# Columns 32 to 39 of the chunk rows: a second fetch from DRAM against a copy by ScalarE

## The chip, the cores and the metric

The kernel runs on one core of one Trainium2 chip. The metric is the device time of one execution in microseconds (us), the median of the runs that were timed. The core has five engines with an instruction stream each: TensorE (PE, with its weight loads as PEld), VectorE (DVE), ScalarE (ACT), GpSimd (POOL) and SyncE (SP). Each works through its own stream in order; an instruction that waits for another engine, or for a DMA, holds up all that stands behind it in its stream. SP computes nothing here: it issues nearly all of the DMAs.

## The reference

Two parts follow each other: a linear-attention recurrence over 768 steps with a 40 by 40 state for each of 4 x 8 heads, and a two-layer block on its output.

```python
for t in range(S):                       # S = 768, for every batch b and head h
    y[:, :, t] = np.einsum('bhd,bhde->bhe', rt, state)
    Sa = np.einsum('bhde,bhe->bhd', state, at)
    state_decay = state * wt[:, :, None, :] - np.einsum('bhd,bhe->bhde', Sa, bt)
    state = state_decay + np.einsum('bhd,bhe->bhde', vt, kt)
x = y.transpose(0, 2, 1, 3).reshape(B * S, H * D)      # 3072 x 320
h = x @ w_in                                            # 320 x 2048
g = np.where(h >= 1, h, np.where(h <= -1, 0.0, (h + 1) ** 2 / 4))
out = g @ w_out                                         # 2048 x 320
```

## The kernel before

**Recurrence in chunks.** The 768 steps are cut into 24 chunks of 32 (`L = 32`, `D = 40`, 32 heads). Everything that a chunk needs stands in one row of 240 numbers for each head and step in a DRAM scratch, `scr`: r, v, k, the running decay P, a and b, 40 columns each (`O_R`, `O_V`, `O_K`, `O_P`, `O_A`, `O_B`). There are six scratch tensors, for 128 steps (a set of four chunks) each. For the first two sets the rows are made at the start (`early_rows`, `early_store`), for the others by `prelude` in the background, in four parts a set: ScalarE copies (`wz`, `arena`), VectorE scans, GpSimd products, and a DMA of 640 KB from `arena` to `scr`, after which the next part may write `arena` again.

**From rows to columns.** The products want the 40 numbers of a row on 40 partitions. VectorE transposes blocks of 32 by 32, so 40 numbers take two blocks: columns 0 to 31 of a block of 40 go to partitions 0 to 31, and columns 32 to 39 to partitions 32 to 39. For that, `load_rows` puts each row into SBUF twice. The 32 steps of the heads with f = 0 lie on partitions 0 to 31, and once more on partitions 32 to 63, there from column 32 on, so that the same 32-column window of the tile that shows columns 0 to 31 on the first 32 partitions shows columns 32 to 63 on the next. The heads with f = 1 lie likewise on partitions 64 to 95 and 96 to 127. That makes four DMAs a call: for each f one of n columns (q = 0), and one of n - 32 columns (q = 1). `load_ti` calls it for the tile `ti` (columns 0 to 199 of 16 heads, so a half chunk, `hb` 0 or 1; two tiles, one for each `hb`) and `ab_set` for columns a and b of all 32 heads, from set 2 on (tile `tiab`, and for set 2 `lw` as a second buffer).

**The consumers.** `turn(c, hb, part)` transposes `ti` into `cg` (L464), `ev` (L467) and `pr` (L469). `ab_set` transposes into `ea` (L328), whose products (L337) ScalarE copies to `pairs` (L343); `invert(s)` makes of them the inverses that set s needs.

**The order.** The main loop runs over the chunks. A pass has four parts; each begins with `stage` calls (one step of the chain of a half chunk: L519, L523; L529, L536, L540; L545 to L569; L585, L587, L575) and ends with `fill()`. `fill` hands out, by fixed rates written at the top, MoE matmuls (`feed`: first layer L631, gate L639 to L642, split L648 and L649, second layer L661), the conversion of the weights (`wgen`) and the background (`rows`, `ab`, `inv`, by the table WINDOWS). So each engine's stream is fixed when the program is built. `load_ti(c + 2, 0)` stands in the last part of pass c, and `turn(c + 2, 0, 0)` in the second part of pass c + 1; for hb = 1 load and turn are half a pass apart as well.

```python
    def load_ti(c, hb):
        drain("rows", c // 4)
        tis[c, hb] = tih[hb]
        load_rows(tih[hb], c, 0, 200, 16 * hb, 16)
```

`pad_rows` zeroes, on ScalarE, the 32 columns at the end of the second copies, which no DMA writes: of both `ti` tiles at the start, and of `tiab` before set 2.

Of the kernel before, what the change touches and what calls it, by code (L numbers as in the profile page):

```python
# [22 lines left out]
RW = 240  # L23
# [31 lines left out]
def rwkv_moe_kernel(ctx: ExitStack, tc: tile.TileContext, r, k, v, w, a, b, w_in, w_out, ident_d, mask_d, out):  # L55
    nc = tc.nc
# [29 lines left out]
    tiab = const.tile([128, 16, 80], F32, name="tiab")  # L86
# [31 lines left out]
    def zero(x, row=0):  # L118
        z = zero_c[row : row + x.shape[0]]
        nc.scalar.copy(x, (z if len(x.shape) == 2 else z.unsqueeze(1)).broadcast_to(list(x.shape)))  # L120

    def pad_rows(x, n):
        for q in (1, 3):
            zero(x[32 * q : 32 * q + 32, :, n : n + 32], 32 * q)

    def init_cg(i, part):
        cg, pr = cgs[i], prs[i]
# [175 lines left out]
    def load_rows(dst, c, off, n, h0=0, nh=NH):  # L303

        sc = scr[c // 4]
        for f in range(2):
            for q in range(2):
                row = (h0 + f) * 128 + 32 * (c % 4)
                m = n - 32 * q
                src = bass.AP(  # L310
                    sc.tensor, sc.offset + row * RW + off + 32 * q, [[RW, 32], [256 * RW, nh // 2], [1, m]]
                )
                nc.sync.dma_start(dst[64 * f + 32 * q : 64 * f + 32 * q + 32, :, 0:m], src)  # L313

    def ab_set(s):

        if s == 2:
            pad_rows(tiab, 48)
        bufs = [tiab, lw[:, 0:1280].rearrange("p (h x) -> p h x", x=80)] if s == 2 else [tiab]
        for c in range(4 * s, 4 * s + len(bufs)):  # L320
            load_rows(bufs[c % len(bufs)], c, O_A, 80)
        yield AB_W[5]
        for c in range(4 * s, 4 * s + 4):
            tv = bufs[c % len(bufs)].rearrange("p h (j x) -> p h j x", x=40)[:, :, :, 0:32]
            for half in range(2):
                ea = work.tile([128, 8, 2, 32], F32, tag="ea", name="ea")
                for i in range(2):
                    nc.vector.transpose(ea[:, 4 * i : 4 * i + 4], tv[:, 8 * half + 4 * i : 8 * half + 4 * i + 4])  # L328
                    yield AB_W[0]
                yield AB_W[1]  # L330
                ps = psum()[:, 0:128]
                for p in range(8):
                    for f in range(2):
                        rows = slice(64 * f, 64 * f + D)
                        q = 2 * f + p % 2
                        sl = p // 2
                        nc.tensor.matmul(  # L337
                            ps[32 * q : 32 * q + 32, 32 * sl : 32 * sl + 32],
                            lhsT=ea[rows, p, 0, :], rhs=ea[rows, p, 1, :], start=True, stop=True,
                        )  # L340
                assert s - 1 in turned_in
                at = 256 * (c % 4) + 128 * half
                nc.scalar.copy(pairs_f[:, at : at + 128], ps)  # L343
                yield AB_W[2] + AB_W[3]
            if c + len(bufs) < 4 * s + 4:
                load_rows(bufs[c % len(bufs)], c + len(bufs), O_A, 80)
            if c < 4 * s + 3:
                yield AB_W[4] // len(bufs)
# [26 lines left out]
    def adopt(s):  # L375

        drain("inv", s)
        W = lw[:, 1024:2048]
        nc.vector.transpose(tinv.rearrange("p c h i -> p i (c h)"), W.rearrange("p (a i) -> p i a", i=32))
        turned_out.add(s)  # L380
# [50 lines left out]
    tis = {}  # L431
# [5 lines that stand above are left out]
# [16 lines left out]

    quarter = lambda f, i: slice(64 * (1 - f) + 32 * i, 64 * (1 - f) + 32 * i + 32)
    order = [4 * (n % 2) + n // 2 for n in range(8)]

    def turn(c, hb, part):
        u = 2 * c + hb
        cg, pr = cgs[u % 3], prs[u % 3]
        t5 = tis[c, hb].rearrange("p h (j x) -> p h j x", x=40)[:, :, :, 0:32]  # L460
        if part == 0:
            for f in range(2):
                rows = slice(64 * f, 64 * f + 64)
                nc.vector.transpose(cg[rows, f::2, C_X : C_X + 32], t5[rows, :, 4, :])  # L464
        elif part == 1:
            evs[u] = work.tile([128, 8, 2, 32], F32, tag="ev", name="ev")
            nc.vector.transpose(evs[u], t5[:, :, 1:3, :])  # L467
        else:
            nc.vector.transpose(pr[:, :, :, 8:40], t5[:, :, 0:4:3, :])  # L469

    def scores(c, hb, parts=(0, 1)):
        u = 2 * c + hb
        for part in parts:
            (score_products, score_masks)[part](u)
# [223 lines left out]
    def weight_tile(k, t):  # L698
        kind, j, i, _ = jobs[k]
        if kind:  # L700
            if w2_pool[j // 8 ^ 1] is None:
                open_w2(j // 8 ^ 1)
            return w2_pool[j // 8 ^ 1].tile([128, 2, 320], t, name=f"w2_{j}", tag=f"w2_{j}")
        return w1_tile(j, i, t)

    def raw_load(k):
        raws[k] = weight_tile(k, F32).rearrange("p b n -> p (b n)")
        x, at = raws[k].bitcast(I32), 0
        for src in jobs[k][3]:
            m = src.shape[0]  # L710
            nc.gpsimd.dma_start(x[at : at + m], src.bitcast(I32))
            at += m
# [52 lines left out]
    def pull(gen, n=1):  # L765
        for _ in range(n):
            if next(gen, "end") == "end":
                return False
        return True
# [15 lines left out]
    pad_scr(0)  # L785
    early_load(1)
    for x in tih:
        pad_rows(x, 168)
    for i in (0, 2):
        init_cg(i, 0)  # L790
    for i in range(2):
# [24 lines left out]
    at = lambda n, f: todo.setdefault(n, []).append(f)  # L816
# [3 lines left out]
        at(1, lambda i=i: copy_rv(0, i, 1, 3))  # L820
    for k in range(AHEAD):
        at(2, lambda k=k: raw_load(k))
    at(10, lambda: [turn(0, 0, j) for j in (1, 2, 0)])
    at(11, lambda: scores(0, 0, (0,)))
    at(14, lambda: load_ti(1, 0))
    at(18, lambda: scores(0, 0, (1,)))
    at(19, lambda: turn(0, 1, 0))
    i = 0
    while done.get("inv", -1) < 0:
# [15 lines left out]
    row = lambda: next(rows_of[1])  # L845
# [9 lines left out]
    def feed(cols):  # L855

        if not Xs:
            return
        owed[0] += cols * (not idle[0])
        while owed[0] > 0:  # L860
            d = next(mgen)
            owed[0] = 0 if d is None else owed[0] - d
            idle[0] = d is None

    def stage(c, hb):

        if (c, hb) in gens:
            next(gens[c, hb], 0)

    def catch_up():  # L870

        for f in deferred:
            f()
        deferred.clear()

    def fill():

        catch_up()
        for k in range(6):
            feed(1280)  # L880
            if first:
                first.pop(0)()
            due[0] += PACE[now[0] >= 25]
            while due[0] > 0:
                pull(wgen)
                due[0] -= 1
            background(now[0] + 10 / SLOTS * (k + 1) / 6)
        now[0] += 10 / SLOTS

    for c in range(NC + 1):  # L890
        nxt = c + 1 < NC
        if c < NC:
            gens[c, 0] = chain(c, 0)
            gens[c, 1] = chain(c, 1)
        stage(c - 1, 1)
        stage(c, 0)
        if c < NC:
            if c and c % 4 == 0:
                adopt(c // 4)
            for j in (1, 2):  # L900
                turn(c, 1, j)
        fill()
        stage(c - 1, 1)
        stage(c, 0)
        if c < NC:
            scores(c, 1)
        if nxt:
            load_ti(c + 1, 1)
        if nxt:
            load_cg(c + 1, 0)  # L910
            turn(c + 1, 0, 0)
        fill()
        for g, (t0, nt) in enumerate(groups):
            if t0 + nt == 32 * c:
                Xs[g] = relayout(g)
                if idle[0]:
                    owed[0], idle[0] = -TRAIL * 3072, False
        if c == NC:
            break
        stage(c, 0)  # L920
        stage(c, 1)
        if nxt:
            for j in (1, 2):
                turn(c + 1, 0, j)
        fill()
        stage(c, 0)
        stage(c, 1)
        if c + 2 < NC:
            load_ti(c + 2, 0)
        if nxt:  # L930
            scores(c + 1, 0)
            load_cg(c + 1, 1)
            turn(c + 1, 1, 0)
        fill()
# [33 lines left out]
```

## Time and profile before

| | before |
|---|---|
| time, median of 3 runs | 857.49 us (856.85 to 858.71) |
| the profiled execution's own time | 856.34 us |
| its span, first to last instruction | 854.3 us |
| busy: PE / PEld / DVE / ACT / POOL | 81% / 74% / 69% / 49% / 52% |
| mean granted TensorE clock | 0.876 |

A busy share is an average over the whole span, and this kernel has stages with different limits. PE is busy with the chain of the recurrence from the start, and with the two layers from about a fifth of the span on; at the end only the two layers are left.

### The profile page before, as it was taken

The page shows a single profiled execution, that of the slowest core. Times are in us where ns is not written, and L with a number is a line of the kernel's source. Part 1 is how long each engine was busy: PE and PEld are TensorE (multiplying, and loading weights), DVE is VectorE, ACT ScalarE, POOL GpSimd, SP SyncE. Part 2 cuts the span into 40 slices and gives each one's busy share as a digit, 9 for nine tenths or more (in the row PEclk, how much of TensorE's full clock was granted, in tenths as well). Part 3 has the DMA queues.
Part 4 walks back from the last instruction along what each step waited for, and adds up shares of the span by engine and source line. Part 5 has one row for each costly group of instructions (what it writes and reads, how often), then busy time and mean ns, then how long its engine had stood idle before and what let it go on. Part 6 is the DMA issues. An engine that isn't in the chain of part 4 may idle for free.

```text
span 854.3 us, 35432 instructions
## 1 busy us (share of the span) xinstructions
PE 693.4 (81%) x15360; PEld 635.2 (74%) x15360; DVE 592.0 (69%) x1338; ACT 417.4 (49%) x888; POOL 441.5 (52%) x621
## 2 busy tenths in 40 slices
PE   4325755686588876988998899999999999999994
PEld 4224645576477765877887789988898899998994
DVE  6895689978566855778777697777777677676210
ACT  6306455456434533445454455455554555555552
POOL 0300278986334677934678457864258643222331
PEclk9565555789877977879999799999999999999998
DMA  9999599987799575995769967756455445450100
GB/s 292 189 197 236 94 198 190 223 194 180 153 166 197 133 158 92 198 191 139 157 141 181 188 163 155 142 117 129 94 103 97 105 92 132 100 108 19 36 16 16
DMA packets 221459, 122.01 MB, mean 143 GB/s; under 512 B 142144, under 2 KB 214016, under 8 KB 221304
## 3 DMA queue, kind: packets, MB, share of 16 engines
q1 hardware_dynamic: 215032, 98.12, 56.9%
q0 software_dynamic: 6272, 21.63, 9.4%
q8 instruction: 121, 1.98, 1.0%
q14 instruction: 34, 0.28, 0.1%
HBM read 90.54 MB, written 27.53 MB: 138 GB/s over the span
## 4 chain that ended last, share of the span: by engine, by line
PE 41%; DVE 16%; DMA 15%; POOL 9%; SPq 6%; ACT 6%; issue 5%; ACTq 0%; DVEq 0%; POOLq 0%
PE ph L631 13%; PE po L661 12%; DMA ti<-scr 4%; SPq L313 4%; PE p L556 3%; DMA scr<-arena 3%; PE p L545 2%; POOL lw L371 2%; POOL lw L365 2%; DMA scr<-in_r_dram 2%; PE p L585 2%; PE p L529 2%; PE p L485 2%; PE p L519 2%; PE p L203 1%
## 5 line engine op out<-in xcount | busy, mean ns | idle before, releaser
L649 POOL TENSOR_TENSOR gl<-gt,gh 128x512 fp32r<-128x512 f32 x96 | 123.9, 1290 | 207.3 <-ACT gh L648 206.1
L631 PE MATMUL ph<-X,w 120*128 120x256 f32 x1536 | 221.4, 299 | 2.3 <-issue 1.7
L631 PEld LDWEIGHTS ph<-X,w 120*128 120x128 f32 x1536 | 201.1, 201 | 9.3 <-issue 2.3
L661 PE MATMUL po<-w,gh 128*128 128x320 f32 x768 | 135.5, 319 | 17.7 <-ACT gh L648 17.5
L642 DVE SCALAR_TENSOR_TENSOR gt<-gt,ph 128x512 f32<-128x512 f32 x96 | 65.7, 684 | 102.4 <-ACT gt L640 89.7
L661 PEld LDWEIGHTS po<-w,gh 128*128 128x128 f32 x768 | 117.4, 193 | 21.4 <-ACT gh L648 20.4
L540 ACT ACTIVATE cg<-p 32x160 f32<-32x160 f32 x192 | 56.5, 295 | 89.5 <-PE p L529 60.0
L639 ACT ACTIVATE gt<-ph,half_c 128x512 f32<-128x512 f32 x96 | 66.1, 688 | 65.3 <-PE ph L631 65.2
L661 PE MATMUL po<-w,gl 128*128 128x320 f32 x384 | 79.0, 330 | 18.0 <-POOL gl L649 18.0
L563 DVE SCALAR_TENSOR_TENSOR cg<-p,pr 40x160 f32<-40x160 f32 x184 | 59.1, 321 | 49.5 <-PE p L556 47.6
L371 POOL TENSOR_TENSOR lw<-lw 128x31 f32<-128x31 f32 (+15 forms) x155 | 87.2, 562 | 9.4
L365 POOL TENSOR_TENSOR lw<-lw 128x31 f32<-128x31 f32 (+15 forms) x155 | 82.1, 530 | 8.9
L497 DVE TENSOR_TENSOR cg<-p,mask 32x256 f32<-32x256 f32 x192 | 80.6, 420 | 3.5
L661 PEld LDWEIGHTS po<-w,gl 128*128 128x128 f32 x384 | 63.0, 199 | 22.5 <-POOL gl L649 22.1
L556 PE MATMUL p<-cg 128*64 128x72 f32 (+1 forms) x1536 | 65.1, 243 | 2.0 <-issue 2.0
L648 ACT CAST gh<-gt 128x512 fp32r<-128x512 f32 x96 | 59.6, 621 | 10.5 <-DVE gt L642 9.5
L640 ACT ACTIVATE gt<-gt 128x512 f32<-128x512 f32 x96 | 60.7, 632 | 3.1
L556 PEld LDWEIGHTS p<-cg 128*64 128x64 f32 x1536 | 59.3, 151 | 2.6 <-issue 2.6
L550 ACT COPY ss<-p 40x320 f32<-40x320 f32 x92 | 38.6, 419 | 43.8 <-PE p L545 42.0
L585 PEld LDWEIGHTS p<-pr,ss 40*40 40x40 f32 x1472 | 37.1, 133 | 30.0 <-issue 21.9
L536 DVE SCALAR_TENSOR_TENSOR cg<-p,mask 32x128 f32<-32x128 f32 x192 | 55.3, 288 | 5.9 <-PE p L529 0.7
L585 PE MATMUL p<-pr,ss 40*40 40x32 f32 x1472 | 42.2, 213 | 20.9 <-DVE pr L469 17.2
(95 smaller groups left out, 1060.3 us busy)
## 6 DMA issues: line engine op xcount, KB each, us to landing
ti<-scr SPq DMA_DIRECT2D x96, 200.0 KB
ti<-scr SPq DMA_DIRECT2D x96, 168.0 KB
scr<-arena POOLq DMA_DIRECT2D x16, 640.0 KB, 6.8
cg<-scr SPq DMA_DIRECT2D x96, 80.0 KB
X<-Y SPq DMA_DIRECT2D x36, 160.0 KB
scr<-wide SPq DMA_DIRECT2D x8, 640.0 KB
w<-in_moe_w_out_dram POOLq DMA_DIRECT2D x16, 320.0 KB, 5.3
tiab<-scr SPq DMA_DIRECT2D x28, 160.0 KB
```

The source lines that it names most:

```text
L365: eng.tensor_mul(t3, W3[:, 0:n, j : j + 1].broadcast_to([128, n, m]), L3[:, j + 1 :, j].unsqueeze(1).broadcast_to([128, n, m]),)
L371: eng.tensor_sub(W3[:, 0:n, j + 1 :], W3[:, 0:n, j + 1 :], t3)
L497: nc.vector.tensor_tensor(out=cg[q, f::2, C_X : C_X + 64][:, 4 * i : 4 * i + 4].rearrange("p h (j x) -> p h j x", x=32), in0=ps[quarter(f, ...
L556: nc.tensor.matmul(psv[h // 8][64 * f : 64 * f + 64, h // 2 % 4, 0:n3], lhsT=cgw[:, h * CW + C_G : h * CW + C_G + 64], rhs=cg[:, h, C_R : ...
L585: nc.tensor.matmul(psv[er[f], p, :], lhsT=ss[er[f], p, :], rhs=pn[er[f], p, 0, 8:40], start=True, stop=True)
L631: nc.tensor.matmul(phs[k % 2][:, n * j : n * j + n], lhsT=wt[0, f // 4, wi // 2][:, wi % 2, fs], rhs=Xs[g][:, xi, :], start=i == 0, stop=i ...
L639: nc.scalar.activation(gt, ph, AF.Relu, bias=half_c, scale=0.5)
L640: nc.scalar.activation(gt, gt, AF.Square)
L642: nc.vector.scalar_tensor_tensor(out=gt, in0=gt, scalar=1.0, in1=ph, op0=ALU.min, op1=ALU.max)
L648: nc.scalar.copy(gh, gt)
L649: nc.gpsimd.tensor_sub(gl, gt, gh.bitcast(F32))
L661: nc.tensor.matmul(pos[i], lhsT=x[:, ts_], rhs=w, start=q == 0 and k == 0, stop=end)
```

## The change

`load_rows` issues two DMAs instead of four: the fetches of n - 32 columns (q = 1) are gone. A new helper, `shift_rows`, lets ScalarE copy columns 32 to 39 of every block of 40 from partitions 0 to 31 to columns 0 to 7 on partitions 32 to 63, and from 64 to 95 to 96 to 127: two instructions a loaded tile, of 32 partitions by 40 runs of 8 numbers for `ti` (5 blocks x 8 heads) and 32 runs of 8 for `tiab` and `lw`. For `ti` they stand in the first and third part of a pass, between `fill()` and the `stage` calls; for `tiab` and `lw` right before the transposes. `pad_rows` is gone; GpSimd zeroes both `ti` tiles once at the start.

```diff
-    def pad_rows(x, n):
-        for q in (1, 3):
-            zero(x[32 * q : 32 * q + 32, :, n : n + 32], 32 * q)
...
         for f in range(2):
-            for q in range(2):
-                row = (h0 + f) * 128 + 32 * (c % 4)
-                m = n - 32 * q
-                src = bass.AP(
-                    sc.tensor, sc.offset + row * RW + off + 32 * q, [[RW, 32], [256 * RW, nh // 2], [1, m]]
-                )
-                nc.sync.dma_start(dst[64 * f + 32 * q : 64 * f + 32 * q + 32, :, 0:m], src)
+            row = (h0 + f) * 128 + 32 * (c % 4)
+            src = bass.AP(sc.tensor, sc.offset + row * RW + off, [[RW, 32], [256 * RW, nh // 2], [1, n]])
+            nc.sync.dma_start(dst[64 * f : 64 * f + 32], src)
+
+    def shift_rows(x):
+
+        x = x.rearrange("p h (j x) -> p h j x", x=40)
+        for f in range(2):
+            nc.scalar.copy(x[64 * f + 32 : 64 * f + 64, :, :, 0:8], x[64 * f : 64 * f + 32, :, :, 32:40])
...
-        if s == 2:
-            pad_rows(tiab, 48)
...
         for c in range(4 * s, 4 * s + 4):
+            shift_rows(bufs[c % len(bufs)])
...
+    def shift(c, hb):
+        shift_rows(tis[c, hb])
...
     for x in tih:
-        pad_rows(x, 168)
+        nc.gpsimd.memset(x, 0.0)
...
+    at(9, lambda: shift(0, 0))
     at(10, lambda: [turn(0, 0, j) for j in (1, 2, 0)])
...
     at(18, lambda: scores(0, 0, (1,)))
+    at(17, lambda: shift(0, 1))
...
         fill()
+        if nxt:
+            shift(c + 1, 0)
         stage(c - 1, 1)
...
         fill()
+        if nxt:
+            shift(c + 1, 1)
         stage(c, 0)
```

In ScalarE's stream, late in the program (pass 22, first part to second part; `gt` is the gate, `Y` the rounded output of the recurrence, `cg` the operand tile of a half chunk), before:

```order
L639 ACTIVATE gt<-ph_64,half_c 128x512
L640 ACTIVATE gt<-gt 128x512
L575 CAST Y<-yt 128x2x4x32
L540 ACTIVATE cg_87<-p_12557 32x4x40 x2
L540 ACTIVATE cg_87<-p_12556 32x4x40 x2
```

and after:

```order
L639 ACTIVATE gt<-ph_64,half_c 128x512
L640 ACTIVATE gt<-gt 128x512
L311 COPY ti_82<-ti_82 32x40x8 x2
L575 CAST Y<-yt 128x2x4x32
L540 ACTIVATE cg_87<-p_12553 32x4x40 x2
L540 ACTIVATE cg_87<-p_12552 32x4x40 x2
```

The two copies stand behind the gate and ahead of the rounding of Y and of the four evictions into `cg`.

In SP's stream, the loads that `ab_set` of set 2 issues first, and what stands ahead of them and behind (X is the input tile of the first layer, `ld_w` an input of `prelude`), before:

```order
L605 DMA X_2929<-Y 40x1024 x3
L611 DMA X_2929<-Y 40x2x256 x2
L614 DMA X_2929<-Y 40x2x256
L313 DMA tiab<-scr_107 32x16x80
L313 DMA tiab<-scr_107 32x16x48
L313 DMA tiab<-scr_107 32x16x80
L313 DMA tiab<-scr_107 32x16x48
L313 DMA lw<-scr_107 32x16x80
L313 DMA lw<-scr_107 32x16x48
L313 DMA lw<-scr_107 32x16x80
L313 DMA lw<-scr_107 32x16x48
L261 DMA ld_w<-in_w_dram 128x1x320
```

and after:

```order
L605 DMA X_2925<-Y 40x1024 x3
L611 DMA X_2925<-Y 40x2x256 x2
L614 DMA X_2925<-Y 40x2x256
L305 DMA tiab<-scr_107 32x16x80 x2
L305 DMA lw<-scr_107 32x16x80 x2
L257 DMA ld_w<-in_w_dram 128x1x320
```

The order is the same; the second DMA of `tiab` and all that follows has moved up by the fetches that are gone.

In ScalarE's stream at the last chunk of set 3's `ab_set`, before:

```order
L648 CAST gh<-gt 128x512
L269 COPY wz<-ld_w 128x8x40
L343 COPY pairs<-p_5445 128x128
L343 COPY pairs<-p_5466 128x128
L279 COPY arena<-ld_w 128x8x40
```

and after:

```order
L648 CAST gh<-gt 128x512
L265 COPY wz<-ld_w 128x8x40
L311 COPY tiab<-tiab 32x32x8 x2
L340 COPY pairs<-p_5439 128x128
L340 COPY pairs<-p_5460 128x128
L275 COPY arena<-ld_w 128x8x40
```

The copies of `tiab` come in between the split and the eviction of the products that read the transposed `tiab`.

## Rows read from the trace of the kernel before

**Rows 1.** Three stretches: each engine's busy us, TensorE clock, DMA share, GB/s
```profile
0.00:200.00 200.00, 106.76 (x2903) 95.66 (x2904) 156.77 (x329) 96.23 (x196) 96.15 (x160) 0.68 0.92 202
200.00:500.00 300.00, 250.66 (x5419) 226.42 (x5422) 208.96 (x471) 138.51 (x305) 180.39 (x245) 0.87 0.77 159
500.00:800.00 300.00, 293.12 (x6725) 271.04 (x6726) 218.42 (x529) 159.59 (x350) 149.08 (x206) 1.00 0.52 108
```

**Rows 2.** SP's DMA queue (packets, MB, share), issues (count, KB each, us to landing)
```profile
q1 hardware_dynamic: 215032, 98.12, 56.9%
...
ti<-scr SPq DMA_DIRECT2D x96, 168.0 KB
scr<-arena POOLq DMA_DIRECT2D x16, 640.0 KB, 6.8
...
tiab<-scr SPq DMA_DIRECT2D x28, 96.0 KB
```

**Rows 3.** ScalarE by line and shape: count, busy us, mean ns of one, idle before
```profile
L540 ACT ACTIVATE cg<-p 32x160 f32<-32x160 f32 x192 | 56.5, 295 | 89.5 <-PE p L529 60.0 <-DVE cg L536 27.7
...
L269 ACT COPY wz<-ld_w 128x320 f32<-128x320 f32 x16 | 12.6, 787 | 9.9 <-DMA ld_w<-in_w_dram 7.8 <-POOL arena L296 2.2
L279 ACT COPY arena<-ld_w 128x320 f32<-128x320 f32 x16 | 12.5, 783 | 35.2 <-DVE ld_w L245 16.6 <-DMA scr<-arena 14.9 <-DVE dz L278 3.8
...
L743 ACT CAST w<-X 128x320 fp32r<-128x320 f32 x16 | 7.2, 448 | 0.0
```

**Rows 4.** Timeline of all engines, late: start, duration, instruction, [idle before, releaser]
```profile
756.79 0.39 ACT L575 CAST Y<-yt 128x256 fp32r<-128x256 f32 x1
...
758.72 0.60 ACT L540 ACTIVATE cg<-p 32x160 f32<-32x160 f32 x2 [1.54 <-PE p L529]
...
761.94 0.91 DVE L464 STREAM_TRANSPOSE cg<-ti 64x256 f32<-64x256 f32 x2
```

**Rows 5.** Timeline of SP: the load that this transpose reads
```profile
743.16 1.78 SPq L313 DMA_DIRECT2D ti<-scr  x4
```

**Rows 6.** Pieces of the chain that ended last: start, us, what
```profile
228.73 3.54 DMA tiab<-scr
...
250.16 2.93 SPq L313
...
254.67 6.04 DMA lw<-scr
...
408.19 7.86 DMA ti<-scr
...
465.42 8.60 DMA scr<-arena
```

**Rows 7.** Timeline of PE: the waits at four places
```profile
233.09 0.68 PE L337 MATMUL p<-ea 40*32 40x32 f32 x32 [8.23 <-DVE ea L328]
...
261.34 0.76 PE L337 MATMUL p<-ea 40*32 40x32 f32 x32 [3.51 <-DVE ea L328]
...
387.31 0.56 PE L337 MATMUL p<-ea 40*32 40x32 f32 x32 [1.52 <-DVE ea L328]
...
477.88 1.51 PE L661 MATMUL po<-w,gh 128*128 128x320 f32 x8 [2.05 <-ACT gh L648]
```

**Rows 8.** Timeline of ScalarE at four places
```profile
214.22 0.60 ACT L540 ACTIVATE cg<-p 32x160 f32<-32x160 f32 x2 [0.20 <-DVE cg L536]
...
256.68 0.79 ACT L269 COPY wz<-ld_w 128x320 f32<-128x320 f32 x1
...
385.78 0.77 ACT L269 COPY wz<-ld_w 128x320 f32<-128x320 f32 x1
...
474.09 0.81 ACT L279 COPY arena<-ld_w 128x320 f32<-128x320 f32 x1 [4.01 <-DMA scr<-arena]
```

**Rows 9.** Timeline of SP around the longest store
```profile
463.43 4.61 SPq L313 DMA_DIRECT2D tiab<-scr  x4
468.08 3.27 SPq L313 DMA_DIRECT2D ti<-scr  x4
```

## The prediction

> **What bounds the kernel now.** I read the stretches first, then the DMA table, then the waits at single places, because the change trades one resource (DMA and SP's issue slots) for another (ScalarE).
>
> The stretches [rows 1] show three different kernels. From 500 to 800 us PE is busy 293.12 of 300 us at full clock: 6.9 us are idle, and the DMA engines stand at a share of 0.52. Nothing that shortens a transfer can win more there than those 6.9 us. From 200 to 500 us PE idles 300 - 250.66 = 49.3 us with DMA at 0.77, and from 0 to 200 us it idles 200 - 106.76 = 93.2 us with DMA at 0.92. PE's stream is fixed and ends the span, so an idle us that goes away before 500 us is a us off the end. In the first stretch, though, VectorE is busy 156.77 of 200 us: it runs the first inverse, the early rows and the weights, and PE mostly waits for it. So I look for gains from 200 to 500 us, where the busiest engine next to PE has 30% idle and PE's waits end with single late events.
>
> **What is removed.** 96 fetches of 168 KB for ti, and 28 + 4 of 96 KB for tiab and lw (the lw ones have the same shape) [rows 2]: 16,128 + 3,072 = 19,200 KB of the 98.12 MB on SP's queue [rows 2], a fifth. Each also took an issue slot of SP: a load of four takes 1.78 us when SP is not held up [rows 5], so about 0.45 us a fetch and some 57 us of SP's time over the span. What matters is where a load is late for somebody.
>
> *The ti loads are not late.* The load issued at 743.16 [rows 5] is read by a transpose at 761.94 that shows no idle time before it [rows 4], 17 us after the issue ended. The longest that a ti load takes to land on the chain is 7.86 us [rows 6]. Making it shorter wins nothing by itself.
>
> *The tiab and lw loads are late*, at two places. (1) PE waits 8.23 us at 233.09 for the transpose of tiab [rows 7]; the last of the four fetches is issued at 228.73 and lands 3.54 us later [rows 6], at 232.27. Now the second one is the last, two slots (0.98 us) earlier; if the data are the limit, it lands up to another 1.2 us earlier, since 320 of 512 KB are fetched. Then come two copies (0.8 us, below) before the transpose. Gain 0.98 - 0.8 = 0.2 to 1.4; I take 0.5, since a good part of the 3.54 us has to pass in any case. (2) PE waits 3.51 us at 261.34 [rows 7]. SP is held up on the second fetch of lw for 2.93 us, and the fourth, issued at 254.67, lands 6.04 us later [rows 6], at 260.71. Now the second is the last: issued from 250.16 to 253.09, landed between 256.2 and 259.1 if it takes the same 6.04 us from the start or from the end of its issue. ScalarE is free for the copies at 257.5, behind L269 [rows 8]. So the transpose begins at 258.4 to 260.0 instead of 260.8. Gain 0.8 to 2.4; I take 1.7.
>
> *The stores of arena are late too*, since the loads share the DMA engines with them. The chain holds one of 8.60 us at 465.42 [rows 6], against a median of 6.8 [rows 2]. ScalarE waits 4.01 us for it (L279), and PE then 2.05 us for the split [rows 8, 7]. A tiab and a ti load are issued into just that stretch [rows 9], and 2 x 96 + 2 x 168 = 528 KB of them go; at the mean rate of that stretch, 159 GB/s [rows 1], that is 3.4 us of transfer. Of PE's 2.05 us I take 2.0 (bounds 0 and 2.05). Over the whole span L279 waits 14.9 us for stores [rows 3], so 10.9 us at other places. A fifth of that would be 2.2 us; not every such wait reaches PE, so I take 1.0 (0 to 2.2).
>
> **What is added: ScalarE's copies.** 96 of 32 partitions by 320 numbers and 32 by 256. The trace has no copy with runs of 8. The nearest rows are on both sides: L743, contiguous, 320 numbers, 448 ns, and L269, which writes with a step of 10 numbers, 787 ns for the same count [rows 3]. I take 0.45 us for ti and 0.40 for tiab (L575, 256 numbers, 0.39 [rows 4]), as eight neighbouring numbers are closer to contiguous than single ones; that is 96 x 0.45 + 32 x 0.40 = 56 us on an engine that is busy 49%. Both ends stay for the range.
>
> The Trainium skill (SBUF — State Buffer, section on door 1, the DMA port swizzle) says that SBUF accesses stay at full bandwidth within a line of 16 bytes, four fp32, and that each move to a new line costs. L269 against L743 agrees: 787 against 448 ns. By that rule a run of 32 bytes fills whole lines, and the copies cost what L743 costs; by row L269 alone they would cost 0.34 us more each, 128 x 0.34 = 43 us more of ScalarE's time.
>
> *What hides the ti copies.* They stand behind the gate and ahead of Y and the evictions L540. Late in the program ScalarE waits 1.54 us ahead of L540, for PE [rows 4], and 89.5 us over the 48 groups [rows 3], 1.9 each. A pair of 0.9 us fits into that; what it delays is the rounding of Y, which nobody waits for at once. Where the cover is thin, as at 214.22 (0.20 us [rows 8]), L540 and the split behind it come up to 0.7 us later, and PE's second layer waits for the split. I count 0.3 in all (0 to 3, if four or five such places pass all of it on). Behind ScalarE's copies VectorE's transposes wait; the pair is done about 1 us after the gate (756.8), 4 us before the transpose at 761.94 [rows 4].
>
> *What does not hide.* The tiab copies stand right before the transposes. At the last chunk of set 3 ScalarE comes free at 386.55 (L269 [rows 8]), and PE waits at 387.31 for a transpose [rows 7] that takes about 0.45 us and so began near 386.8. With two copies in between it begins near 387.4: 0.65 us lost (0 to 1.3, the latter with copies of 0.8). At the other chunks I take 0 (0 to 1), because PE's waits at L337 are few.
>
> *The zeroing.* ScalarE loses four small copies at the start and two before set 2; GpSimd gains two memsets before the first load, when it is idle (busy 96 of the first 200 us [rows 1]). I count 0 for both; without that cover it would be at most 8 us, once (2 x 1,600 numbers at L269's 2.5 ns each).
>
> **The sum.** 0.5 + 1.7 + 2.0 + 1.0 = 5.2 us gained, 0.3 + 0.65 = 0.95 lost, net 4.25. The profiled execution took 856.34 us, 2.0 around its span of 854.3, and lies 1.15 below the median of 857.49. From the median: **853.2 us**. With all lower ends of the gains (0.2 + 0.8 + 0 + 0) and all upper ends of the losses (3 + 1.3 + 1) it is 861.8; with the reverse, 8.05 of gains and no loss, 849.4.
>
> **The rivals.**
> - *The queue is the pace.* If the idle time of PE before 500 us hangs on the DMA backlog more widely than at the four places (shares of 0.92 and 0.77 speak for it, VectorE's 78% before 200 us against it), a fifth fewer bytes on SP's queue would take up to a fifth of 142.5 us, 28 us. Half of that gives 843.
> - *Nothing measurable.* The late loads wait for the landing, not for bytes, and the copies give back what is left: places (1) and (2) at their lower ends, the stores unchanged, the losses at 0.95. That is 857.5. For it: the fetch at 228.73 needs 3.54 us although its 96 KB are 0.6 us at 159 GB/s. Against it: the store of 8.60 us beside loads against 6.8.
> - The Trainium skill (DMA: Bandwidth & Descriptors, "Anatomy of one DMA — SWDGE (gpsimd) path") gives this rival its rule: about 2 us of a DMA are fixed, most of it the receipt of the last write, whatever its size. By that rule two of the 3.54 us stay and place (1) wins little; the row does not contradict it.
> - *Slower: copies at the price of L269.* A pair then costs 1.57 us, which is more than the 1.54 us of cover late in the program: from 0.77 us a copy on, the ti copies push L540, the split and PE's second layer. If a quarter of the 48 half chunks pass on 0.6 us (7 us) and the tiab copies lose 1.3 at two places instead of 0.65 at one (2.6), against 4 us of gains, it ends at 863. Lines of 16 bytes speak against it; the untried shape speaks for it.
>
> **How the numbers follow.** 0.2% of the time is 1.7 us, about what a measurement of this kernel can tell from no change. Chances: my forecast (gains over 1.7 up to 9 us) 0.46, the queue as the pace 0.12, nothing measurable 0.22, slower 0.20. Faster by over 0.2% is 0.58, within 0.22, slower 0.20. The forecast's own range is 849.4 to 855.7. The range for 8 in 10 is 846 to 860.5: it leaves out most of the first rival and the far half of the last.
>
> **What would show it.** Right: ti transposes still without idle time; L311 copies of ti near 450 ns; the idle time before L540 shrunk by about 0.9 us a group and the split no later against PE; PE's wait at the first tiab little changed, that at lw shorter; shorter waits of L279 for stores; PE's idle time from 500 to 800 us still near 7 us. Wrong: copies near 0.8 us; ScalarE waiting at L311 for a landing, with the gate behind it; or PE's idle time before 200 us, which I left alone, moving by more than 3 us either way. That last would mean that I misjudged what VectorE and PE wait for at the start.

## The result, and the profile after

The changed kernel takes 849.0 us, median of 12 runs (844.61 to 854.87), against 857.46 for the kernel before in the same comparison (12 runs, 852.47 to 864.78): a ratio of 0.9899, 95% interval 0.9864 to 0.9934, or 8.7 us less. The forecast was 853.2, so 4.25 us less. Repeated later (experiment after_again) the ratio is 0.9903 [0.9872, 0.9934].

Single runs of one kernel spread over some 10 us here, and the profiled executions with them. Before: 856.34 us, span 854.3. After: 853.33 us, span 851.4, which is 4 us above its median. After, second profile: 847.19 us, span 845.2. So I read both profiles after and trust what they share.

The profile page of after, busy time by engine and the chain that ended last by engine:

```profile
PE 694.7 (82%) x15360; PEld 639.7 (75%) x15360; DVE 592.5 (70%) x1338; ACT 477.5 (56%) x1010; POOL 444.8 (52%) x623
...
PE 49%; POOL 7%; DVE 6%; DMA 3%; ACT 3%; issue 2%; SPq 1%; ACTq 0%; POOLq 0%; DVEq 0%
```

The same chain before:

```profile
PE 41%; DVE 16%; DMA 15%; POOL 9%; SPq 6%; ACT 6%; issue 5%; ACTq 0%; DVEq 0%; POOLq 0%
```

DMA and SP's queue go from 21% of the chain to 4% (5% in the second profile), and "issue", in which an engine waits for nothing that the profile shows, from 5% to 2%. ScalarE is busy 60 us more, 56.7 of it the copies (56 forecast).

SP's queue and the store of arena, after (answers to [rows 2]):

```profile
q1 hardware_dynamic: 172024, 78.45, 42.3%
...
scr<-arena POOLq DMA_DIRECT2D x16, 640.0 KB, 5.6
```

The queue moves a fifth less, and the store, whose bytes did not change, lands after 5.6 us (6.1 in the second profile) instead of 6.8. ScalarE by line and shape, after (answers to [rows 3]):

```profile
L540 ACT ACTIVATE cg<-p 32x160 f32<-32x160 f32 x192 | 56.6, 295 | 40.1 <-PE p L529 22.1 <-DVE cg L536 15.8
...
L311 ACT COPY ti<-ti 32x320 f32<-32x320 f32 x96 | 43.8, 456 | 2.2
...
L275 ACT COPY arena<-ld_w 128x320 f32<-128x320 f32 x16 | 12.6, 785 | 30.4 <-DVE ld_w L241 18.5 <-DMA scr<-arena 11.8
...
L311 ACT COPY tiab<-tiab 32x256 f32<-32x256 f32 x28 | 11.3, 403 | 6.6 <-DMA tiab<-scr 5.9
```

The copies cost 456 and 403 ns, where I took 450 and 400. They used up more than half of the idle time ahead of L540: 89.5 before, 40.1 now. L275, the L279 of before, waits 11.8 us for stores instead of 14.9.

The three stretches, after (answers to [rows 1]):

```profile
0.00:200.00 200.00, 107.60 (x2901) 97.20 (x2902) 155.30 (x328) 104.07 (x211) 98.97 (x162) 0.69 0.78 184
200.00:500.00 300.00, 250.33 (x5403) 227.61 (x5405) 210.21 (x472) 165.89 (x363) 180.51 (x245) 0.87 0.60 133
500.00:800.00 300.00, 296.86 (x6771) 275.70 (x6766) 219.41 (x529) 185.34 (x402) 150.41 (x206) 0.99 0.35 81
```

The DMA shares fall from 0.92, 0.77 and 0.52 to 0.78, 0.60 and 0.35. From 500 to 800 us PE idles 3.1 us (3.9 in the second profile) instead of 6.9, which I had not expected.

PE at the four places of [rows 7], and at one place more (355.51), after:

```profile
232.95 0.67 PE L334 MATMUL p<-ea 40*32 40x32 f32 x32 [7.56 <-DVE ea L325]
...
258.48 0.77 PE L334 MATMUL p<-ea 40*32 40x32 f32 x32 [4.02 <-DVE ea L325]
...
355.51 0.75 PE L529 MATMUL p<-x,tinv 32*32 32x72 f32 x17 [2.72 <-issue]
...
357.20 3.78 PE L631 MATMUL ph<-X,w 120*128 120x256 f32 x16
...
389.98 0.67 PE L334 MATMUL p<-ea 40*32 40x32 f32 x32 [2.22 <-DVE ea L325]
...
478.93 1.44 PE L661 MATMUL po<-w,gh 128*128 128x320 f32 x8 [2.10 <-ACT gh L648]
```

The first place won 0.7 us. At lw PE starts 2.9 us earlier, though its wait is longer. The last chunk of set 3 lost 0.70 (1.52 to 2.22), and the store's place won nothing: 2.10 instead of 2.05. At 355.51 an issue stall of 2.72 us stands where before had 1.07. The second profile of the same kernel:

```profile
232.78 0.67 PE L334 MATMUL p<-ea 40*32 40x32 f32 x32 [7.40 <-DVE ea L325]
...
258.42 0.77 PE L334 MATMUL p<-ea 40*32 40x32 f32 x32 [3.87 <-DVE ea L325]
...
385.54 0.56 PE L334 MATMUL p<-ea 40*32 40x32 f32 x32 [2.22 <-DVE ea L325]
...
475.30 1.34 PE L661 MATMUL po<-w,gh 128*128 128x320 f32 x8
```

Here the stall is absent and PE does not wait for the store's split at all. So those two differ between executions of one kernel, and the three other places repeat to 0.2 us.

### The profile page after: what moved, and what is told of

Read it like the earlier page. It is cut to its first block, busy times and chain, and to the rows that moved or that the text cites. A ratio compares the mean times of both kernels' runs of the same rounds, so it can differ in the third digit from the quotient of the medians.

```text
span 851.4 us, 35341 instructions
## 1 busy us (share of the span) xinstructions
PE 694.7 (82%) x15360; PEld 639.7 (75%) x15360; DVE 592.5 (70%) x1338; ACT 477.5 (56%) x1010; POOL 444.8 (52%) x623
## 3 DMA queue, kind: packets, MB, share of 16 engines
q1 hardware_dynamic: 172024, 78.45, 42.3%
q8 instruction: 121, 1.98, 1.0%
## 4 chain that ended last, share of the span: by engine, by line
PE 49%; POOL 7%; DVE 6%; DMA 3%; ACT 3%; issue 2%; SPq 1%; ACTq 0%; POOLq 0%; DVEq 0%
PE ph L631 16%; PE po L661 15%; PE p L556 4%; PE p L545 3%; PE p L585 3%; PE p L485 2%; PE p L529 2%; PE p L519 2%; POOL lw L368 2%; POOL lw L362 2%; POOL gl L649 2%; PE p L334 1%; DMA lw<-scr 1%; DMA ld_w<-in_w_dram 1%; DMA scr<-arena 1%
## 5 line engine op out<-in xcount | busy, mean ns | idle before, releaser
L631 PE MATMUL ph<-X,w 120*128 120x256 f32 x1536 | 222.8, 300 | 1.3 <-issue 1.3
L631 PEld LDWEIGHTS ph<-X,w 120*128 120x128 f32 x1536 | 202.3, 202 | 8.1 <-issue 1.3
L639 ACT ACTIVATE gt<-ph,half_c 128x512 f32<-128x512 f32 x96 | 66.0, 688 | 65.3 <-PE ph L631 64.9
L368 POOL TENSOR_TENSOR lw<-lw 128x31 f32<-128x31 f32 (+15 forms) x155 | 88.5, 571 | 9.4
L362 POOL TENSOR_TENSOR lw<-lw 128x31 f32<-128x31 f32 (+15 forms) x155 | 82.7, 533 | 8.9
L540 ACT ACTIVATE cg<-p 32x160 f32<-32x160 f32 x192 | 56.6, 295 | 40.1 <-PE p L529 22.1
L556 PE MATMUL p<-cg 128*64 128x72 f32 (+1 forms) x1536 | 66.4, 245 | 0.4 <-issue 0.4
L648 ACT CAST gh<-gt 128x512 fp32r<-128x512 f32 x96 | 59.6, 621 | 10.5 <-DVE gt L642 9.5
L536 DVE SCALAR_TENSOR_TENSOR cg<-p,mask 32x128 f32<-32x128 f32 x192 | 55.3, 288 | 10.2 <-PE p L529 2.6
L556 PEld LDWEIGHTS p<-cg 128*64 128x64 f32 x1536 | 60.6, 154 | 0.9 <-issue 0.9
```

Of the source, the lines that this page charges most:

```text
L362: eng.tensor_mul(t3, W3[:, 0:n, j : j + 1].broadcast_to([128, n, m]), L3[:, j + 1 :, j].unsqueeze(1).broadcast_to([128, n, m]),)
L368: eng.tensor_sub(W3[:, 0:n, j + 1 :], W3[:, 0:n, j + 1 :], t3)
L556: nc.tensor.matmul(psv[h // 8][64 * f : 64 * f + 64, h // 2 % 4, 0:n3], lhsT=cgw[:, h * CW + C_G : h * CW + C_G + 64], rhs=cg[:, h, C_R : ...
L631: nc.tensor.matmul(phs[k % 2][:, n * j : n * j + n], lhsT=wt[0, f // 4, wi // 2][:, wi % 2, fs], rhs=Xs[g][:, xi, :], start=i == 0, stop=i ...
L639: nc.scalar.activation(gt, ph, AF.Relu, bias=half_c, scale=0.5)
L648: nc.scalar.copy(gh, gt)
```

## The experiments

All ratios are against the kernel before on the same chip, whose median there was 857.46 us (for after), 859.34 (e1 to e4), 858.37 (e5 to e8) and 858.56 (after_again, e9 to e11); so compare ratios and not times. In diffs, minus is the changed kernel and plus the experiment; "..." marks lines left out.

| run | fetches | copies | us | ratio | 95% interval |
|---|---|---|---|---|---|
| after / after_again | all halved | all, ScalarE | 849.0 / 848.25 | 0.9899 / 0.9903 | 0.9864 to 0.9934 / 0.9872 to 0.9934 |
| e1_ti_only | ti halved | ti | 854.19 | 0.9952 | 0.9929 to 0.9975 |
| e2_ab_only | tiab, lw halved | tiab, lw | 851.26 | 0.9910 | 0.9875 to 0.9944 |
| e3_fetch_and_copy | all twice | all | 861.9 | 1.0038 | 1.0010 to 1.0066 |
| e4_no_copy | all halved | none | 844.46 | 0.9837 | 0.9796 to 0.9878 |
| e5_tiny_second | halved, plus tiny ones | all | 850.84 | 0.9916 | 0.9888 to 0.9943 |
| e6_copy_twice | all halved | all, twice | 866.18 | 1.0098 | 1.0062 to 1.0135 |
| e7_copy_ab_only | all halved | tiab, lw | 845.55 | 0.9856 | 0.9818 to 0.9894 |
| e8_copy_ti_only | all halved | ti | 845.81 | 0.9860 | 0.9826 to 0.9893 |
| e9_ab_on_vector | all halved | ti ScalarE, tiab, lw VectorE | 859.76 | 1.0014 | 0.9993 to 1.0034 |
| e10_ti_on_vector | all halved | ti VectorE, tiab, lw ScalarE | 878.6 | 1.0251 | 1.0222 to 1.0279 |
| e11_both_on_vector | all halved | all, VectorE | 888.98 | 1.0369 | 1.0334 to 1.0405 |

**One part of the change alone: e1_ti_only and e2_ab_only.** In e1 tiab and lw are fetched twice and not copied, and `pad_rows` is back for tiab:

```diff
+            for q in range(2 if n == 80 else 1):
+                m = n - 32 * q
...
-            shift_rows(bufs[c % len(bufs)])
```

> Only the ti loads are halved and copied by ScalarE; tiab and lw are fetched twice as before. Theory A (bytes: the second fetches lie in the way of stores and other loads on the shared DMA engines): 16.1 of the 19.2 MB go, so most of the 8.5 us comes here, 850 to 852 us. Theory B (late loads: only the shorter tiab and lw loads matter): ratio to before 0.997 to 1.000, 855 to 857.5 us.

In e2 ti is fetched twice and not copied:

```diff
+            for q in range(2 if n == 200 else 1):
+                m = n - 32 * q
...
-        shift_rows(tis[c, hb])
+        return
```

> Only tiab and lw are halved and copied; the ti loads are fetched twice as before. Theory A: 3.1 of 19.2 MB go, and the copies cost 0.65 us at the last chunk of set 3, so 855 to 857.5 us. Theory B: most of the gain is here, 850 to 853 us.

Both halves win: e2 7.7 us, e1 4.1 us (of 857.5). Their sum, 11.8, is more than the 8.7 of the whole change; the intervals (some 2 to 3 us each) do not show whether the two share something or simply add up. The forecast gave shorter ti loads nothing of themselves; their bytes stood only in the terms for the stores.

**The gain alone and the cost alone: e4_no_copy and e3_fetch_and_copy.** e4 leaves out columns 32 to 39 of the transposed rows:

```diff
-        for f in range(2):
+        for f in range(0):
```

> Half the fetches and no copies; columns 32 to 39 of every block are left out of the products. The gain of the DMAs alone. If the copies are hidden, 847.5 to 849.5 us, like the changed kernel less about 1 us. If the copies eat a part of the gain, 846 us or less.

e3 fetches everything twice and copies over it:

```diff
+            for q in range(2 if True else 1):
+                m = n - 32 * q
```

> All four fetches stay, and ScalarE writes the same numbers over them: the price of the copies alone (56 us of ScalarE's time, and a second link between a load and its transpose). If the idle time before L540 hides them, 857 to 859 us (0 to +1.5, mostly the tiab copies). If they cost more than I thought and the DMA gain is that much larger, 860 us or more.

The fetches alone are worth 1.63%, 14.0 us (10.5 to 17.5 by the interval), where the forecast had 5.2 with an upper bound of 8.05. The copies cost 3.3 us (0.9 to 5.7) beside full fetches, and 0.9901 (the mean of after and after_again) - 0.9837 = 0.0064, 5.5 us, beside halved ones, where the forecast had 0.95. That second difference carries an uncertainty of about 4 us, but e7 and e8 below lie between its ends. At lw, without copies (e4):

```profile
252.52 0.65 PE L334 MATMUL p<-ea 40*32 40x32 f32 x32 [2.35 <-DVE ea L325]
```

This wait was 3.87 and 4.02 us with the copies ahead of the transposes.

**Bytes or number of DMAs: e5_tiny_second.** Each removed fetch comes back as a DMA of 32 numbers, so SP issues as many as before:

```diff
+            tiny = bass.AP(sc.tensor, sc.offset + row * RW + off + 40, [[RW, 32], [1, 1]])
+            nc.sync.dma_start(dst[64 * f + 32 : 64 * f + 64, 0, 8:9], tiny)
```

> The changed kernel with two more DMAs a load, of 32 numbers each, to cells that no result reads: SP's issue slots and the number of DMAs are those of before, the bytes those of the changed kernel. If bytes are what is won, 849 to 851 us, like the changed kernel. If it is slots and landings (a load is as late as its last DMA, and SP is held up for each), 855 to 858 us, like before.

0.9916 against 0.9899 and 0.9903: 1.3 us apart, with some 3 us of uncertainty, so over the whole span no difference that this can tell. Some 85% of the gain, and about half at the least, is in what the fetches carried and not in their number. That is 19.2 of 98 MB, and the packets with them: SP's queue has 215,032 before, 178,168 in e5 and 172,024 in the changed kernel. No run here separates bytes from packets. At the lw place the number counts. PE there, e5:

```profile
261.18 0.76 PE L336 MATMUL p<-ea 40*32 40x32 f32 x32 [6.80 <-DVE ea L327]
```

With as many DMAs as before the matmuls start at 261.18, as before (261.34), and not at 258.4. So there the number of issues counts, as the forecast's step on lw said; its 2.7 us are within what the ratios leave open.

**How much cover there is: e6_copy_twice.**

```diff
-        for f in range(2):
+        for f in (0, 1, 0, 1):
```

> The changed kernel with every copy made twice: 56 us more of ScalarE's time at the same places. The copies cost some 3.3 us where the fetches stay (ratio 1.0038) and 5 us where they go (0.9837 against 0.9899). If each us of copies passes on the same share, 853 to 855 us. If the idle time before L540 is used up by the first pair (1.54 us against 0.91), the second costs more than the first: 860 us or above.

The second pair costs 0.0197, 17 us, three times the first. By line and shape, e6:

```profile
L311 ACT COPY ti<-ti 32x320 f32<-32x320 f32 x192 | 87.5, 456 | 4.6
...
L540 ACT ACTIVATE cg<-p 32x160 f32<-32x160 f32 x192 | 56.7, 295 | 12.7 <-PE p L529 5.3 <-DVE cg L536 4.1
L536 DVE SCALAR_TENSOR_TENSOR cg<-p,mask 32x128 f32<-32x128 f32 x192 | 55.2, 288 | 27.8 <-ACT cg L540 22.9 <-PE p L529 1.0
```

The idle time ahead of L540 is down to 12.7 us, and VectorE's L536, which alternates with L540, now waits 22.9 us for ScalarE. With one pair (second profile of after):

```profile
L536 DVE SCALAR_TENSOR_TENSOR cg<-p,mask 32x128 f32<-32x128 f32 x192 | 55.2, 288 | 8.6 <-ACT cg L540 2.5 <-PE p L529 1.0
```

This is the mechanism of the rival "copies at the price of L269", at a price that the copies do not have.

**Which copies cost: e7_copy_ab_only and e8_copy_ti_only.** All fetches halved; e7 leaves out columns 32 to 39 of ti, e8 those of tiab and lw:

```diff
     def shift(c, hb):
-        shift_rows(tis[c, hb])
+        return
```

> All loads halved; only tiab and lw are copied, ti is not (columns 32 to 39 of r, v, k, P, a as read by the turns are left out). If the ti copies cost the 5 us between the changed kernel and the one with no copies, 845 us; if the tiab copies do, 849 us.

```diff
         for c in range(4 * s, 4 * s + 4):
-            shift_rows(bufs[c % len(bufs)])
```

> All loads halved; only ti is copied, tiab and lw are not (columns 32 to 39 of a and b are left out of the pair products from set 2 on). If the tiab copies, which stand right between a load and its transposes, cost the 5 us, 845 us; if the ti copies do, 849 us.

One group of copies alone costs 1.6 us (0.9856 against 0.9837) or 2.0 us (0.9860), both together 5.5. The differences are within the intervals; the order is the one that a shared cover would give, which is not more than a hint. Two pairs with the same copies also price the fetches: e8 against e1, the 3.1 MB of tiab and lw, 0.0092 or 7.9 us (intervals apart); e7 against e2, the 16.1 MB of ti, 0.0054 or 4.6 us (intervals overlapping).

**The same again, and the copies on VectorE: after_again, e9, e10, e11.**

> The change as it is, once more, for a second profile of it. Theory: the ratio is again near 0.990 (0.986 to 0.994), and PE's idle time and granted clock differ between the two profiles of one program at single places from 340 to 400 us (the first profile had an idle gap of 2.72 us at 355.51 that nothing released, and a clock of 0.79 in that stretch). If the gap and the clock of 0.79 are there again, they belong to the change and are part of what the copies cost; if they are gone, they are an accident of one execution.

It repeats to 0.0004, and the stall is gone; the clock from 340 to 400 us is 0.86, as before the change. So neither comes with every execution of the change. Nor is the stall its own: e1, e2, e3, e9 and e11 have one of 2.1 to 2.6 us at the same instruction (last section).

```diff
-            shift_rows(bufs[c % len(bufs)])
+            shift_rows(bufs[c % len(bufs)], nc.vector.tensor_copy)
```

> The copies of tiab and lw are made by VectorE, right ahead of its own transposes, those of ti stay on ScalarE. Theory (the copies cost time by being queued in ScalarE between work that PE waits for, and by the hand-over to VectorE): most of the cost of the tiab copies is gone, and the ratio comes near that of the run without them, 0.986 to 0.988. Rival (the transposes come later by the copy's own time, whoever makes it): 0.990, as with ScalarE.

```diff
-        shift_rows(tis[c, hb])
+        shift_rows(tis[c, hb], nc.vector.tensor_copy)
```

> The copies of ti are made by VectorE, those of tiab and lw stay on ScalarE. Theory (as before: the cost is ScalarE's lateness for Y, the evictions L540 and the split): 0.986 to 0.988, near the run without ti copies. Rival (VectorE, busy 70%, is the next to be late, since it evicts and transposes for every half chunk): 0.991 or more, slower than with the copies on ScalarE.

> All copies are made by VectorE. Theory: what is left of the cost of the copies, 5 us on ScalarE, is at most 2 us, ratio 0.984 to 0.987, the fastest correct version. Rival (VectorE is late instead, its 56 us more come between the transposes that PE waits for before 500 us): 0.990 to 0.996.

My theory fell in all three: 1.0014, 1.0251 and 1.0369. In e10 the rival held (0.991 or more); e9 and e11 lie above their rivals' ranges too. By line and shape, e10:

```profile
L540 ACT ACTIVATE cg<-p 32x160 f32<-32x160 f32 x192 | 56.7, 295 | 125.8 <-DVE cg L536 65.3 <-PE p L529 59.1
...
L311 DVE COPY ti<-ti 32x320 f32<-32x320 f32 x96 | 48.0, 500 | 3.0
```

and e9:

```profile
L311 DVE COPY tiab<-tiab 32x256 f32<-32x256 f32 x28 | 15.3, 546 | 7.2 <-DMA tiab<-scr 6.4
```

A copy costs VectorE 500 ns (ti) and 546 ns (tiab), against 456 and 403 on ScalarE. In e10 L540 now waits 65.3 us for VectorE instead of 15.8, and e10 is already 8.9 us later than before at half chunk 9 (table below). VectorE, not ScalarE, is the engine without cover there. In e9 VectorE waits itself for the landing of tiab, 6.4 us, but that is nothing new. Before:

```profile
L328 DVE STREAM_TRANSPOSE ea<-tiab 128x256 f32<-128x256 f32 x56 | 21.3, 416 | 19.1 <-DMA tiab<-scr 14.6 <-PE p L337 4.3
```

What e9 loses against the changed kernel (some 10 us) has no cause shown; in its one profile 8.7 us go between the 15th and the 18th half chunk, with a stall of 2.6 us among them. So taking away the hand-over between engines does not win back the cost of the copies, and ScalarE is the cheaper place of the two.

## Why the prediction was half right

The direction held, and 849.0 lies in the range (the forecast's own, 849.4 to 855.7, misses it by 0.4). But two sizes were wrong, and partly cancelled. The table gives the start of the copy into x (L523), one for each half chunk, counted from 0: before in us, then how much earlier (minus) or later each other profile reaches it.

```
half chunk   before   after  again  no copies  e10   forecast by then
 9           221.93   +0.8   +0.8     -3.5     +8.9     0
11           275.30   -3.6   -3.0     -9.1     +5.9    -2.2
23           476.91   +1.0   -3.5    -10.1    +18.1    -2.25
25           508.86   +0.8   -6.5    -12.9    +18.0    -4.25
end          844.67   -2.9   -9.1    -15.2    +26.0    -4.25
```

(In the forecast, other stores, 1.0, and lost cover, 0.95, are taken as spent by the 23rd. The last row is the end of ScalarE's last copy.)

**The first tiab place (0.5): right.** PE's wait of 8.23 fell to 7.56 and 7.40.

**The lw place (1.7, 0.8 to 2.4): right in kind, 2.9 measured, above its bounds.** The matmuls start at 258.48 and 258.42 instead of 261.34. My sign for it, a shorter wait, failed: PE arrives there 3.4 us earlier, in large part because of a stall that I had not counted. Before, at 250.41:

```profile
250.41 1.34 PE L556 MATMUL p<-cg 128*64 128x72 f32 x17 [2.02 <-issue]
```

The second profile of after, at the same 17 matmuls:

```profile
247.51 0.78 PE L556 MATMUL p<-cg 128*64 128x72 f32 x17 [0.65 <-issue]
```

The stall shrank from 2.02 to 0.65 (0.37 in the first profile), and the matmuls behind it take 0.78 instead of 1.34 us. The time that lw itself won is the step's own, SP's shorter queue, as e5 shows.

**The store at 465 (2.0): about right in size, and not in every execution.** From the 23rd to the 25th half chunk the first profile wins 0.3 us, the second 3.0. The experiments say which is usual: e4 to e9, all with halved fetches and no copies of ti on VectorE, win 2.1 to 2.9. e2, with only tiab and lw halved, wins 3.0, e1, with only ti, 0.6, and e3 nothing (one profile each), which points to the tiab load more than to ti. What the wait is worth is more than its length. PE before, ahead of the wait of 2.05 at 477.88 [rows 7] and behind it:

```profile
473.65 2.18 PE L631 MATMUL ph<-X,w 120*128 120x256 f32 x16
...
485.59 3.78 PE L631 MATMUL ph<-X,w 120*128 120x256 f32 x16
```

PE, second profile of after, at the second of these:

```profile
480.33 2.17 PE L631 MATMUL ph<-X,w 120*128 120x256 f32 x16
```

The same 16 matmuls need 3.78 us behind the wait (2.93 in the first profile) and 2.17 without it. By windows, before and then the second profile of after (the last three columns are granted clock, DMA share, GB/s):

```profile
480.00:490.00 10.00, 9.71 (x214) 8.75 (x215) 6.40 (x17) 2.52 (x8) 5.58 (x8) 0.53 1.02 188
```

```profile
480.00:490.00 10.00, 9.85 (x182) 9.26 (x182) 9.03 (x21) 6.32 (x13) 4.74 (x6) 1.00 0.64 158
```

A granted clock of 0.53 is nearly the lower of the two levels, 1.2 of 2.4 GHz. I priced every wait at its length and none at the slow matmuls after it. But this is no sure gain: in the second profile L631 took 3.78 us at 465.28, behind a wait of 2.74 at 457.72, where the first profile and before, behind the same wait, took 2.17.

**Other stores (1.0).** L275 waits 3.1 us less for stores and the median store is 1.2 or 0.7 us shorter, as forecast in kind. From the 11th to the 23rd half chunk even the kernel without copies wins only 1.0 us.

**Late tiab loads that I did not see: "at two places" was wrong.** I looked for late loads where PE waits. VectorE waits for the landing of tiab at two more places, at 420.54 and, for 2.76 us, at 537.90. VectorE before, and then in e1, where only ti is halved:

```profile
420.54 0.77 DVE L328 STREAM_TRANSPOSE ea<-tiab 128x256 f32<-128x256 f32 x2 [3.89 <-DMA tiab<-scr]
```

```profile
424.31 0.77 DVE L334 STREAM_TRANSPOSE ea<-tiab 128x256 f32<-128x256 f32 x2 [1.15 <-DMA tiab<-scr]
```

SP ahead of it, before and then in e1:

```profile
404.49 4.91 SPq L313 DMA_DIRECT2D ti<-scr  x4
...
413.69 2.68 SPq L313 DMA_DIRECT2D tiab<-scr  x4
```

```profile
410.98 2.10 SPq L313 DMA_DIRECT2D ti<-scr  x2
...
417.90 2.64 SPq L313 DMA_DIRECT2D tiab<-scr  x4
```

The ti load holds SP for 4.91 us, and the tiab load follows 9.2 us behind its start; with ti halved it follows after 6.9. PE, before, passes it on:

```profile
422.79 0.45 PE L337 MATMUL p<-ea 40*32 40x32 f32 x32 [0.66 <-DVE cg L587]
...
424.59 1.44 PE L661 MATMUL po<-w,gh 128*128 128x320 f32 x8 [0.55 <-ACT gh L648]
```

Both waits are gone in e4 and in the second profile of after (where VectorE waits 2.44 us at this place, now for ScalarE's copy), and from the 19th to the 20th half chunk both profiles of after, e1, e2, e4, e5, e7, e8 and e9 win 1.4 to 1.8 us. So a ti load that its own reader never waits for can still reach PE: it holds SP, and the tiab load behind it lands late. The forecast read the ti load at 408.19, with its 7.86 us on the chain [rows 6], as one that costs nothing.

**Nothing moves from 0 to 200 and from 500 to 800 us: wrong for the fetches.** Behind 509 us the two profiles of after win 3.7 and 2.6 us, the kernel without copies 2.3. Of before's short waits there, four are gone in the first profile: issue stalls of 1.07, 0.88 and 0.64 us, and 0.53 us that the profile puts down to a ti load. Ahead of 222 us the kernel without copies wins 3.5 us. Most of that, 2.3, comes between the 6th and 7th half chunk, at one VectorE instruction of the weights' conversion. VectorE before:

```profile
179.02 3.65 DVE L731 SCALAR_TENSOR_TENSOR X<-X 128x320 uint32<-128x320 uint32 x1
```

and without copies (e4):

```profile
177.70 0.49 DVE L731 SCALAR_TENSOR_TENSOR X<-X 128x320 uint32<-128x320 uint32 x1
```

GpSimd before, and then in e4:

```profile
178.50 0.57 POOL L711 DMA_DIRECT2D w<-in_moe_w_out_dram  x1
179.09 0.33 POOL L371 TENSOR_TENSOR lw<-lw 128x60 f32<-128x60 f32 x1
...
181.28 1.04 POOL L296 TENSOR_TENSOR arena<-ld_b,wz 128x320 f32<-128x320 f32 x1
```

```profile
177.39 0.57 POOL L711 DMA_DIRECT2D w<-in_moe_w_out_dram  x1
```

In e4 the instruction begins 0.26 us before GpSimd's DMA issue is over, and takes 0.49 us. Before, it begins 0.05 us before that end and lasts until 182.67, 0.35 us behind the end of GpSimd's run of products at 182.32. With the copies it begins at 179.96 in the second profile, inside that run, and takes 3.23. (In e4 it is the next L731 that is held, for 2.81 us, but by then the first is done.) The Trainium skill (GPSIMD Engine Reference, section 1, Specifications) says that GpSimd shares its SBUF interfaces with VectorE and contends with VectorE instructions of two SBUF inputs, which L731 is; these rows agree. So part of the copies' cost is not their time but the order in which two other engines meet, and the same 2.3 us are part of what e4 shows for the fetches. e7, without ti copies, has 0.49 us there too and e8, with them, has not; that the copies must always lose this meeting is not shown.

**The copies (0.95 lost): right in price, too small in sum.** 456 and 403 ns against 450 and 400: the rule of the Trainium skill that the forecast weighed (SBUF — State Buffer, door 1, lines of 16 bytes) agrees with the rows, and the rival at 787 ns falls. The tiab term is exact at the last chunk of set 3: 0.65 forecast, 0.70 measured twice. What failed is "thin cover, 0.3 in all": e4, e7 and e8 put the cost of all copies at 5.5 us, against an upper bound of 5.3. One such place, VectorE in the second profile, ahead of that L731:

```profile
176.66 0.61 DVE L536 SCALAR_TENSOR_TENSOR cg<-p,mask 32x128 f32<-32x128 f32 x2 [1.04 <-ACT cg L540]
```

Before, this instruction waited for nothing. The other places I can name are lw (about 1.5 us of PE's wait) and set 3 (0.7). With the 2.3 us at L731 these are 4.5 of the 5.5. By the table most of the cost lies ahead of 222 us, where the forecast had little: 4.3 of the 6.1 us between the second profile and e4 are there by the 9th half chunk (1.0 of it from the very start, where other profiles differ by as much either way), all 6.1 by the 11th.

**The step that failed.** "Look for gains where PE's waits end with single late events" of the changed tiles and the store: 5.2 us where e4 shows 14.0. It gave the bytes no other way to reach PE. The traces show two: VectorE's waits behind SP's held-up issues, and stalls in which PE waits for its own instructions (last section). *The queue is the pace*, to which I gave 0.12, would have been 843; the fetches alone give 843.5 by the ratio. Its idea, a backlog that acts more widely, is the nearer one; that its number fits is luck, since the half in it had no row behind it. *Nothing measurable* and *slower* fall with the ratio. What I cannot settle is how the 14 us divide: by table some 6 belong to tiab and lw of set 2, 3 to the store's place, 2 to the stretch behind 509 us and 3 to the one ahead of 222, each from one profile with accidents of 2 to 5 us.

## What to carry to other kernels

A transfer that nobody waits for still has a price where DMA engines are busy: halving the ti fetches, whose readers never waited, was worth about 4 to 5 us (4.1 in e1, with the copies; 4.6 between e2 and e7) beside the 7.9 of the late ones. So follow such a load to what the issuing engine sends next, and look at the waits of every engine on the way to PE and not at PE's alone. Where a change buys one resource with another, run the gain alone and the cost alone before adding them up; two errors of opposite sign can look like a good forecast of the sum. And give added work to the engine with idle time on the chain, not to the one that uses the result: against no copies at all, the same copies cost 5.5 us on ScalarE and 46 on VectorE (1.0369 - 0.9837).

## What was not expected of the hardware

**Stalls in which PE waits for its own instructions.** PE's idle time put down to "issue" behind 190 us, summed over gaps above 0.1 us, in the 14 profiles:

```
ti fetched twice:  before 6.7   e2 7.5   e3 8.4
ti fetched once:   e1 6.3   after 4.7   after_again 3.0   e4 3.1   e5 2.5   e6 1.8
                   e7 3.2   e8 4.1   e9 7.4   e10 3.0   e11 5.1
```

They stand at the same instructions from profile to profile (L631 near 192 us, L556 near 248, L529 near 355) and tend to be shorter with less DMA traffic. At L556 the three profiles with ti fetched twice have 1.6 to 2.0 us, the other eleven at most 0.9; but e9, e11 and the first profile of after each have one of 2.6 to 2.7 us at L529.

No view names a releaser, but the trace's single DMA packets show what PE waits for. On queue q8, which the page calls "instruction", packets of 16,384 bytes arrive through the whole span (1.98 MB). In the 14 profiles, behind 190 us, all 60 of PE's "issue" stalls of over 0.4 us end 1.2 to 1.7 us after such a packet has landed; of matmuls picked at random 6% start at that distance. In the seven profiles with a stall at the L529 near 355 us the packet lands 1.3 to 1.5 us ahead of the matmul, in the seven without 4.1 to 4.5. And the places that stall most are about multiples of 127 matmuls apart (numbers 2884, 3647, 5427 and 8096 of 15,360). By an estimate from 1.98 MB over PE's 30,720 matmuls and weight loads, 64 bytes each, one packet holds just that many with their weight loads. So PE stalls where its next packet of instructions comes late. What makes a packet late is not shown, and the link with the DMA traffic stays a correlation.

**One instruction, 0.49 or 3.65 us**, by whether it starts 0.26 or 0.05 us before GpSimd's DMA issue ends (L731 above).
